# First plan unit by plain block products, six first tiles attended one at a time, later attention begun later

## The chip, the cores and the metric

One NeuronCore of a Trainium2 chip runs the whole program. The metric is the device time of one execution in microseconds (us). Engines have their own instruction queues, each in order: PE (TensorE), ACT (ScalarE), DVE (VectorE), POOL (GpSimd) and SP, which here only issues DMAs.

## What is computed

The reference, cut to what matters:

```python
# attention in chunks of 64 tokens: B=4, H=8, S=576, D=64
scores = scale * np.matmul(q_c, k_c.transpose(0, 1, 2, 4, 3))
scores = scores - np.max(scores, axis=-1, keepdims=True)
attn = np.exp(scores)
attn = attn / (np.sum(attn, axis=-1, keepdims=True) + 1e-09)
out = np.matmul(attn, v_c)
# x: 2304 x 512; four experts, 512 -> 1024 -> 512
for e in range(E):
    h = np.maximum(x @ w1[e], 0.0)
    out += p[:, e:e + 1] * (h @ w2[e])
# normalised by root mean square, then gated: 512 -> 1536 -> 512
g = xn @ w_gate
silu = g * (1.0 / (1.0 + np.exp(-g)))
return (silu * (xn @ w_val) @ w_out)
```

## The kernel before

The 2304 tokens are 18 tiles of 128, in three sets of six. A set is two token blocks of three tiles (384 columns, `NB`). For each set the expert layer runs eight **plan units** (`plan` in the main loop: four experts, two halves of the hidden features each), and after all sets the gated layer runs its units. Below, plan units are numbered through: 0 to 7 belong to set 0, 8 to 15 to set 1, 16 to 23 to set 2. A unit handles two feature pairs `fp`. Each is computed by `hidden` (L654), a Strassen-Winograd scheme over a two by two split of model halves and feature halves and of the two token blocks: seven products instead of eight, out of operands `x0` to `x9` and `w_0` to `w_6` that are sums of blocks. Every product is six matmuls, since each operand is kept as a high and a low part (float32r) and three of the four combinations are used (`PASSES`), for each of two halves of 128 rows. Then `outer` (L753) multiplies the hidden values by `w2`, 72 matmuls, and `flush` adds them up on DVE.

Operands of weights are made on the chip in set 0: `weights` (L301) takes raw w1 blocks, POOL forms sums (`tw`), ACT casts the high part, POOL subtracts to get the low part, and SP stores the result to DRAM for sets 1 and 2, which load it (`w1_load`). w2 is cast and subtracted in every set (`w2p`, four buffers). In sets 1 and 2, `decode` and `prepare` also turn the gated layer's float64 weights into such operands on DVE, POOL and ACT.

Attention handles two tiles at a time, a pair (`attention_unit`, L446): scores on PE into two PSUM banks, `mx` (maximum) and `e` (difference) on DVE, one exponential of 512 columns on ACT for each bank, `rs` (sum and reciprocal) on DVE, `at` (normalised) on POOL, transposition `trA` on PE, copy `aT` on ACT, value products `pv` on PE, copy to `xr`. `x_parts` then casts x operands.

The instructions stand in an order that the program itself works out while it is recorded. Work beside the products are generators ("chains") stepped by `Chains.tick` as the recorded PE time advances; `every` sets how often. Attention of set s+1 is such a chain, added at the start of set s; `norm` of set 0 is added at unit 10. Before unit 0 there is nothing to hide behind: `race` (L104) orders three attention pairs, the first x operands and the first weights by estimated costs in `yield {"ACT": 0.65}, 1` and the like, and fills expected PE idle time with transpositions of the identity into a spare bank (`idle`, dummies, 0.13 us each in its estimate). In it `begin` (L636) computes the two products of block 0 that need no sums; the rest of unit 0 follows when both blocks' operands exist.

## Time and profile before

| | us |
|---|---|
| median of 3 runs | 1272.42 (1272.21 to 1272.92) |
| profiled execution | 1270.46 |
| span in its profile, first to last instruction | 1268.7 |
| PE busy | 1230.4 |
| DVE, POOL, ACT busy | 809.8, 544.5, 413.0 |

The median is over executions without a profile being read; the profiled execution is one more. PE's busy time includes dummies, and matmuls overlap, so the start times in a timeline tell more than the durations.

### The profile page before, as it was taken

Reading aid. Unit: us, or ns where it says so; the run is one execution under the profiler, and the core shown is the slowest. Engines: PE = TensorE matmul, PEld = TensorE weight load, DVE = VectorE, ACT = ScalarE, POOL = GpSimd, SP = SyncE. Lnnn points to the kernel's source line nnn. Section 1 sums busy time; section 2 is a strip of 40 time slices with the busy share of each in tenths; the row PEclk is TensorE's granted clock in tenths of the full one; section 3 lists DMA queues with packets and bytes.
Section 4 is the critical chain, followed back from the end, with each engine's and each line's share of the span. In section 5 each row is a group of like instructions: output and inputs, shape, how many; then the busy total and the mean of one; then the engine's idle time right before and its main releaser. Section 6 shows DMA issues by size and latency. Waiting matters only on the chain. (4 is left out here: it accounts for less than half of the span.)

```text
span 1268.7 us, 20615 instructions
## 1 busy us (share of the span) xinstructions
PE 1230.4 (97%) x7323; PEld 1114.3 (88%) x7323; DVE 809.8 (64%) x1393; ACT 413.0 (33%) x924; POOL 544.5 (43%) x575
## 2 busy tenths in 40 slices
PE   8899999999997999999999999999999999999998
PEld 7788999989887888989998899898988989988997
DVE  6844344456676887767678666896658625763644
ACT  4434333334225232214242223143424232232211
POOL 5567666664345373527356255365204001131100
PEclk9999999999999999999999999999999999999999
DMA  8656555556577587655676766557856746765843
GB/s 285 223 169 218 188 191 181 201 167 205 202 268 239 163 292 261 207 191 213 234 254 204 279 228 229 192 171 303 271 171 239 258 132 224 244 204 200 284 139 125
DMA packets 139782, 274.30 MB, mean 216 GB/s; under 512 B 15648, under 2 KB 15648, under 8 KB 139680
## 3 DMA queue, kind: packets, MB, share of 16 engines
q1 hardware_dynamic: 139680, 272.99, 63.5%
q8 instruction: 58, 0.95, 0.3%
q14 instruction: 44, 0.36, 0.1%
HBM read 210.54 MB, written 62.39 MB: 215 GB/s over the span
## 5 line engine op out<-in xcount | busy, mean ns | idle before, releaser
L763 PE MATMUL o<-w,hh 128*128 128x512 f32 x1584 | 491.5, 391 | 4.0 <-ACT hh L703 2.2
L763 PEld LDWEIGHTS o<-w,hh 128*128 128x128 f32 x1584 | 295.1, 188 | 67.4 <-ACT hh L703 3.8
L763 PE MATMUL o<-w,hl 128*128 128x512 f32 x792 | 310.0, 391 | 1.5 <-DVE hl L200 0.3
L617 PE MATMUL d_ps<-x,w 128*128 128x384 f32 x1008 | 203.8, 338 | 9.8 <-DVE c_ps L201 9.8
L617 PE MATMUL a_ps<-x,w 128*128 128x384 f32 x1008 | 203.3, 337 | 7.3 <-ACT p L665 3.7
L200 POOL TENSOR_TENSOR w<-r,w 128x512 fp32r<-128x512 f32 (+1 forms) x144 | 162.6, 1139 | 103.0 <-ACT w L329 39.5
L617 PE MATMUL c_ps<-x,w 128*128 128x384 f32 x1008 | 203.1, 337 | 0.0
L617 PEld LDWEIGHTS d_ps<-x,w 128*128 128x128 f32 x1008 | 176.0, 188 | 12.9 <-DVE c_ps L201 11.3
L617 PEld LDWEIGHTS a_ps<-x,w 128*128 128x128 f32 x1008 | 176.8, 188 | 11.2 <-ACT p L665 4.3
L763 PEld LDWEIGHTS o<-w,hl 128*128 128x128 f32 x792 | 148.6, 188 | 37.7 <-DVE hl L200 5.3
L200 POOL TENSOR_TENSOR hl<-silu,hh 128x384 fp32r<-128x384 f32 x54 | 55.0, 1043 | 292.0 <-ACT hh L740 291.0
L617 PEld LDWEIGHTS c_ps<-x,w 128*128 128x128 f32 x1008 | 176.4, 188 | 0.2
L940 DVE SCALAR_TENSOR_TENSOR acc<-o,pr,acc 128x512 f32<-128x512 f32 x126 | 94.3, 749 | 126.9 <-PE o L763 126.8
L201 POOL TENSOR_TENSOR w<-w,sc 128x512 f32<-128x512 f32 x36 | 47.6, 1323 | 186.6 <-DVE sc L388 168.7
L200 POOL TENSOR_TENSOR w<-tw,w 128x256 fp32r<-128x256 f32 x112 | 90.8, 820 | 50.0 <-ACT w L233 50.0
L617 PE MATMUL b_ps<-x,w 128*128 128x384 f32 x504 | 101.9, 338 | 0.0
L703 ACT ACTIVATE hh<-c_ps 128x384 fp32r<-128x384 f32 x96 | 47.3, 493 | 158.4 <-DVE c_ps L201 158.3
L201 DVE TENSOR_TENSOR u<-b_ps,p 128x384 f32<-128x384 f32 x84 | 46.4, 553 | 81.9 <-PE b_ps L617 78.9
L201 DVE TENSOR_TENSOR u<-c_ps,u 128x384 f32<-128x384 f32 x84 | 46.7, 556 | 79.0 <-PE c_ps L617 78.5
L665 ACT COPY p<-a_ps 128x384 f32<-128x384 f32 x82 | 39.2, 478 | 165.1 <-PE a_ps L617 165.1
L233 ACT CAST w<-tw 128x256 fp32r<-128x256 f32 x112 | 42.4, 406 | 143.6 <-POOL tw L200 94.4
L617 PEld LDWEIGHTS b_ps<-x,w 128*128 128x128 f32 x504 | 88.9, 189 | 0.1
(98 smaller groups left out, 1349.6 us busy)
## 6 DMA issues: line engine op xcount, KB each, us to landing
w<-wgv SPq DMA_DIRECT2D x252, 256.0 KB, 3.9
w<-w1m SPq DMA_DIRECT2D x224, 256.0 KB, 5.2
r<-in_w SPq DMA_DIRECT2D x128, 256.0 KB, 4.8
w1m<-w SPq DMA_DIRECT2D x112, 256.0 KB, 2.2
wgv<-w SPq DMA_DIRECT2D x84, 256.0 KB, 4.8
raw<-in_wglu SPq DMA_DIRECT2D x36, 512.0 KB, 3.8
w<-wou SPq DMA_DIRECT2D x36, 512.0 KB, 7.3
wou<-q SPq DMA_DIRECT2D x24, 256.0 KB, 4.2
```

Source lines behind the costliest of these rows:

```text
L200: sub = lambda eng, o, a, b: eng.tensor_tensor(o, a, b, op=ALU.subtract)
L201: add = lambda eng, o, a, b: eng.tensor_tensor(o, a, b, op=ALU.add)
L233: nc.scalar.copy(halves(out[n])[:, 0], at[part_of[n]])
L617: nc.tensor.matmul(ps[:, :NB], wv[:, wi, k, :], xs[n][:, xi, k, :], start=(first and k == 0 and m == 0), stop=(last and k == KH - 1 and m ...
L665: nc.scalar.copy(p1, v(a))
L703: nc.scalar.activation(hi, src, AF.Relu)
L763: nc.tensor.matmul(ps, hs[fp, b, j][hx][:, r * P:(r + 1) * P], w2[2 * k + j][:, wi], start=((k, j, m) == (0, 0, 0)), stop=((k, j, m) == last),
L940: nc.vector.scalar_tensor_tensor(out=acc[i], in0=ps, scalar=pr[:, i, e:e + 1], in1=acc[i], op0=ALU.mult, op1=ALU.add,)
```

## The change

In set 0's first unit the eight plain block products replace the seven of the scheme (`plan` unit 0 only): `quarters` casts the four quarters of a raw w1 pair without any sum (POOL subtracts each low part), and `plain` multiplies them with x blocks 0, 1 (token block 0) and 9, 3 (token block 1). Block 0's products stand inside `race`, block 1's after it. `sums_of_first` makes and stores the four operands with sums (5, 4, 6, 3) of these two pairs later, as a chain. The x operands with sums are made by a chain too (`x_rest`), during unit 0's outer products.

The six first tiles are attended one at a time, and their loads are ordered by token block. `first_softmax` takes the maximum times minus the scale as the exponential's bias, straight from PSUM, in eight exponentials of 64 columns a tile, each with the sum over its columns written by ACT (`accum_out`). The value products' result is cast to the x operands' high part straight from PSUM by ACT, the low part is subtracted by DVE, and `xr` is copied behind that. `idle` counts 0.15 us a dummy.

The attention of set 1 begins at unit 1 instead of 0, that of set 2 at unit 12 instead of 8. The remaining hunks pass the pair's width through `attention_unit`, move the old softmax into a function, keep some buffers spare in `race` and let `x9` use `x2`'s buffer.

```diff
+    def quarters(fp, src):
+        last = None
+        for n, k, j in ((0, 0, 0), (1, 1, 0), (7, 0, 1), (2, 1, 1), (None,) * 3):
+            if last is not None:
+                yield {"POOL": 0.75}, 2
+                m, t, at = last
+                sub(nc.gpsimd, t[:, 1], at, t[:, 0].bitcast(F32))
+                parts["plain", fp, m] = t
+                users[id(t)] = 2
+                if m != 7:
+                    users[id(t)] += 1
+                    work.add(store(t, w1m[0][fp][:, m], (0, fp, m)))
+            if n is not None:
+                yield {"ACT": 0.4}, 2
+                t, at = w1p.get(f"w1_{n}"), src[j][:, k * 2 * P:(k + 1) * 2 * P]
+                nc.scalar.copy(t[:, 0], at)
+                last = n, t, at
+    def sums_of_first():
+        for fp in list(kept):
+            def stored(n, t, fp=fp):
+                work.add(store_q(t, halves(t), w1m[0][fp][:, n], (0, fp, n)))
+            yield from operands(kept[fp], tp, stored, (5, 4, 6, 3))
+            tp.put(*kept.pop(fp))
     def weights():
         for s in range(NSET):
-                    for order in () if s > 0 else (ORDER,) if (e, u) != (0, 0) else ((0, 1), (5, 4, 6, 3, 2)):
-                        for fp in own:
-                            key, where = ("moe", s, e, fp), w1m[e][fp]
-                            if order[0] == 0:
-                                kept[fp] = yield from fetched()
-                            def stored(n, t, key=key, where=where):
-                                users[id(t)] = 2
-                                parts[(*key, n)] = t
-                                work.add(store(t, where[:, n], (*key[2:], n)))
-                            yield from operands(kept[fp], w1p, stored, order)
-                            if order[-1] == ORDER[-1]:
-                                tp.put(*kept.pop(fp))
+                    for fp in own if s == 0 else ():
+                        ts = yield from fetched()
+                        if (e, u) == (0, 0):
+                            kept[fp] = ts
+                            yield from quarters(fp, ts)
+                            continue
+                        key, where = ("moe", s, e, fp), w1m[e][fp]
+                        def stored(n, t, key=key, where=where):
+                            users[id(t)] = 2
+                            parts[(*key, n)] = t
+                            work.add(store(t, where[:, n], (*key[2:], n)))
+                        yield from operands(ts, w1p, stored)
+                        tp.put(*ts)
                     for f in range(2 * UF * u, 2 * UF * (u + 1)):
                         raw, = yield from fetched()
                         while not w2p.free():
                             yield
                         t = w2p.get("w2")
+                        yield {"ACT": 0.6}, 1
                         nc.scalar.copy(t[:, 0], raw)
-                        yield
+                        yield {"POOL": 1.3}, 1
                         sub(nc.gpsimd, t[:, 1], raw, t[:, 0].bitcast(F32))
                         tp.put(raw)
 ...
-    def attention_unit(u, loaded=None):
+    def attention_unit(u, loaded=None, done=None):
 ...
+        if done:
+            yield from first_softmax(sc, ex, att[0])
+        else:
+            yield from softmax(sc, ex, att, mx, G, rows, d)
 ...
+        if done:
+            b, t = divmod(u[0] % TPS, TPB)
+            pieces = []
+            for n in range(2):
+                for k in range(2):
+                    x, o = xs[((0, 1), (9, 3))[b][k]], t * P + n * CH
+                    src = ps[n][:, k * KH * CH:(k + 1) * KH * CH].rearrange("p (k n) -> p k n", k=KH)
+                    pieces.append([src, *(x[:, m, :, o:o + CH] for m in range(2))])
+            for n, (src, hi, _) in enumerate(pieces):
+                yield {"ACT": 0.22}, 1 + n
+                nc.scalar.copy(hi, src)
+            for src, hi, lo in pieces:
+                yield {"DVE": 0.22}, len(pieces)
+                sub(nc.vector, lo, src, hi.bitcast(F32))
+            done()
 ...
+    def first_softmax(sc, ex, att):
+        mx, nb, rs = (sm.tile([P, 2, HP], F32, tag=f"f{n}", name=n) for n in ("mx", "nb", "rs"))
+        for h2 in range(2):
+            nc.vector.tensor_reduce(
+                mx[:, h2, :].unsqueeze(2), sc[h2][:, :HP * CH].rearrange("p (g n) -> p g n", n=CH), axis=AX.X, op=ALU.max
+            )
+            yield {"DVE": 0.45 if h2 == 0 else 0.2}, 1
+        nc.vector.tensor_scalar(nb, mx, -SCALE, None, op0=ALU.mult)
+        for h2 in range(2):
+            yield {"ACT": 0.9}, 1
+            for g in range(HP):
+                cols = slice(g * CH, (g + 1) * CH)
+                nc.scalar.activation(
+                    ex[h2][:, cols], sc[h2][:, cols], AF.Exp, scale=SCALE, bias=nb[:, h2, g:g + 1],
+                    accum_out=rs[:, h2, g:g + 1],
+                )
+            banks.put(sc[h2])
+        yield {"DVE": 0.5}, 1
+        nc.vector.tensor_scalar_add(rs, rs, 1e-9)
+        nc.vector.reciprocal(rs, rs)
+        for h2, e in enumerate(ex):
+            yield {"POOL": 0.65}, 1
+            nc.gpsimd.tensor_tensor(
+                att.rearrange("p (hp r n) -> p hp r n", hp=HP, r=2)[:, :, h2, :],
+                e[:, :HP * CH].rearrange("p (g n) -> p g n", n=CH),
+                rs[:, h2, :].unsqueeze(2).to_broadcast([P, HP, CH]),
+                op=ALU.mult,
+            )
+            tp.put(e)
 ...
+    first_w, made_plain = {}, []
+    def plain(fp, b, use, last):
+        for j in range(2):
+            names = ((0, 7), (1, 2))
+            while not banks.free() or any((fp, names[k][j]) not in first_w for k in range(2)):
+                for k in range(2):
+                    key = ("plain", fp, names[k][j])
+                    if key in parts:
+                        first_w[key[1:]] = parts.pop(key)
+                yield {}, 1
+            ps = bank("c_ps")
+            for k in range(2):
+                yield {"PE": 1.1}, 1
+                product(ps, first_w[fp, names[k][j]], ((0, 1), (9, 3))[b][k], k == 0, k == 1)
+            catch_up()
+            if len(made_plain) > 1:
+                yield {"ACT": 0.5}, 2
+                made_plain.pop(0)()
+            made_plain.append(lambda j=j, ps=ps: use(b, j, ps))
+        while last and made_plain:
+            yield {"ACT": 0.5}, 1
+            made_plain.pop(0)()
+            catch_up()
 ...
-        tiles = [attention_tiles(u) for u in own(0)]
-        for u, ts in zip(own(0), tiles):
-            attention_dma(u, ts, (0, 1))
-        for u, ts in zip(own(0), tiles):
-            attention_dma(u, ts, (2,))
+        lead = [[i] for i in range(TPS)]
+        tiles = [attention_tiles(u) for u in lead]
+        for group in (range(TPB), range(TPB, len(lead))):
+            for k in group:
+                attention_dma(lead[k], tiles[k], (0, 1))
             work.step(fetching)
-        first = [attention_unit(u, ts) for u, ts in zip(own(0), tiles)]
+            for k in group:
+                attention_dma(lead[k], tiles[k], (2,))
         nc.sync.dma_start(out=pr, in_=probs)
         nc.sync.dma_start(out=gb, in_=gvec.partition_broadcast(P))
 ...
+        def unit(k):
+            yield from attention_unit(lead[k], tiles[k], lambda: ended.add(k))
+        def block(b):
+            mine = range(TPB) if b == 0 else range(TPB, len(lead))
+            while not all(k in ended for k in mine):
                 yield {}, 1
-            yield from x_sum(n)
-            yield from x_parts(n, eng, True)
-        def two_blocks(t):
-            engines = {5: nc.vector, 4: nc.vector, 6: nc.vector, 3: nc.gpsimd, 2: nc.vector}
-            return [(operand(n, eng), t + 0.8 * m, None) for m, (n, eng) in enumerate(engines.items())]
+            for fp in range(UF) if b == 0 else ():
+                yield from plain(fp, 0, moe_use(fp), fp == UF - 1)
         scratch = banks.get("scratch")
-        waited = []
         def idle(us):
-            for _ in range(int(us / 0.13)):
+            for _ in range(int(us / 0.15)):
                 nc.tensor.transpose(scratch[:, :P], ident, ident)
-        def until():
-            if 5 in xs and all(key in begun for key in early) and not waited:
-                waited.append(True)
-                return True
+        arrive = [3.5, 5.7, 7.6, 14.5, 16.0, 17.5]
+        spared[0] = 5
         gen = work.race(
-            [
-                (first[0], 4.4, None),
-                (first[1], 8.6, lambda t: [(one_block(), t, None)]),
-                (first[2], 12.0, two_blocks),
-            ],
-            (weights(), 15.0, None),
+            [(unit(k), arrive[k], None) for k in range(len(lead))]
+            + [(block(0), 10.0, None), (block(1), 20.0, None)],
+            (weights(), 9.0, None, 0.2),
             idle,
-            until,
         )
+        spared[0] = 0
         banks.put(scratch)
-        x_done()
         feeding = work.add(gen, 0.5)
+        def x_rest():
+            for n in (5, 4, 6):
+                yield from x_sum(n)
+                yield from x_parts(n, nc.vector, True)
+            yield from x_sum(2)
+            while not plain_done:
+                yield
+            yield from x_parts(2, nc.vector, True)
+            x_done()
+        for o in (4, 5, 6, 2):
+            tmp[o] = [tp.get(f"s{o}_{k}") for k in range(KH)]
+        for i in range(TPS):
+            acc[i] = tp.get(f"acc_{i}")
+        plain_done = []
+        resting = work.add(x_rest(), 0.9)
+        work.add(sums_of_first(), 1.6)
 ...
-            if moe and s + 1 < NSET:
-                ahead = work.add(attention(own(s + 1)), first=True)
             for k, (e, fps) in enumerate(plan):
                 end = k == len(plan) - 1
+                if moe and (s, k) == (0, 1) and resting in work.chains:
+                    work.force(resting, lambda: resting not in work.chains)
                 room[0] = 6 if k == 0 else 8 if k >= len(plan) - 2 else 0
+                if moe and (s, k) in ((0, 1), (1, 4)):
+                    ahead = work.add(attention(own(s + 1)), first=True)
 ...
-                    if moe:
+                    if moe and (s, k) == (0, 0):
+                        for _ in plain(fp, 1, moe_use(fp), fp == fps[-1]):
+                            pass
+                        if fp == fps[-1]:
+                            plain_done.append(True)
+                    elif moe:
```

PE from the first products of unit 0; `c_ps`, `a_ps`, `b_ps` are their PSUM banks, `w_n` operand n, `scratch` the dummies. Before:

```order
L617 MATMUL a_ps<-x_534,w_0_361 128x384 x6
L868 MATMUL scratch<-ident 128x128 x5
L617 MATMUL a_ps<-x_601,w_1_410 128x384 x6
L868 MATMUL scratch<-ident 128x128 x13
L617 MATMUL a_ps<-x_534,w_0_464 128x384 x6
L868 MATMUL scratch<-ident 128x128 x5
L617 MATMUL a_ps<-x_601,w_1_523 128x384 x6
L868 MATMUL scratch<-ident 128x128 x13
L617 MATMUL b_ps<-x_689,w_5_592 128x384 x6
```

Now, from the last tile's value products on:

```order
L706 MATMUL c_ps<-x_187,w_0_438 128x384 x6
L706 MATMUL c_ps<-x_188,w_1_634 128x384 x6
L956 MATMUL scratch<-ident 128x128
L706 MATMUL c_ps<-x_187,w_7_711 128x384 x6
L706 MATMUL c_ps<-x_188,w_2_714 128x384 x6
L706 MATMUL c_ps<-x_189,w_0_357 128x384 x6
L706 MATMUL c_ps<-x_190,w_1_403 128x384 x6
L706 MATMUL c_ps<-x_189,w_7_424 128x384 x6
L706 MATMUL c_ps<-x_190,w_2_434 128x384 x6
L706 MATMUL c_ps<-x_189,w_0_438 128x384 x6
L706 MATMUL c_ps<-x_190,w_1_634 128x384 x6
L706 MATMUL c_ps<-x_189,w_7_711 128x384 x6
```

Block 0's four products of the second pair and the eight of block 1 now follow one another with one dummy between them; those of the first pair stand earlier, between the last tiles' transpositions and value products.

ACT from the second weight cast on (`w_0_438` is the first quarter of the second pair, read from `r_0_178`):

```order
L315 CAST w_1_403<-r_0_165 128x256
L315 CAST w_7_424<-r_1_166 128x256
L315 CAST w_2_434<-r_1_166 128x256
L315 CAST w_0_438<-r_0_178 128x256
L560 CAST x_187<-pv_406 128x2x64
L560 CAST x_188<-pv_406 128x2x64
L560 CAST x_187<-pv_407 128x2x64
L560 CAST x_188<-pv_407 128x2x64
L526 COPY aT_445<-trA_440 128x512
L571 COPY xr<-pv_406 128x4x64
L625 ACTIVATE e_426,rs<-sc_383,nb 128x64 x4
L560 CAST x_187<-pv_459 128x2x64
```

and SP's queue around that raw block:

```order
L471 DMA qk_a_156<-in_qkv 128x512
L471 DMA qk_b_157<-in_qkv 128x512
L253 DMA r_0_178<-in_w 128x512
L253 DMA r_1_179<-in_w 128x512
L471 DMA v_152<-in_qkv 128x512
```

The cast of `w_0_438` stands ahead of the second tile's x operands, and its load behind those of the last qk tile.

POOL from unit 0's w2 operands (`w` of 128x512) to unit 1. Before:

```order
L200 TENSOR_TENSOR w_3_876<-tw_629,w_3_876 128x256
L200 TENSOR_TENSOR w_2_925<-r_1_180,w_2_925 128x256
L200 TENSOR_TENSOR w_929<-r_185,w_929 128x512
L200 TENSOR_TENSOR w_952<-r_796,w_952 128x512
L200 TENSOR_TENSOR w_972<-r_798,w_972 128x512
L200 TENSOR_TENSOR w_990<-r_809,w_990 128x512
L509 TENSOR_TENSOR at_921<-e_919,rs_986 128x4x64
L509 TENSOR_TENSOR at_922<-e_919,rs_986 128x4x64
```

Now:

```order
L197 TENSOR_TENSOR w_719<-r_717,w_719 128x512
L197 TENSOR_TENSOR w_772<-r_770,w_772 128x512
L197 TENSOR_TENSOR tw_809<-r_1_166,r_0_165 128x256
L197 TENSOR_TENSOR tw_809<-r_1_166,tw_809 128x256
L197 TENSOR_TENSOR tw_810<-r_1_166 128x256
L197 TENSOR_TENSOR w_901<-r_802,w_901 128x512
L197 TENSOR_TENSOR w_905<-r_804,w_905 128x512
L197 TENSOR_TENSOR tw_925<-r_1_818,r_0_817 128x256
L197 TENSOR_TENSOR tw_925<-r_1_818,tw_925 128x256
L197 TENSOR_TENSOR tw_926<-r_1_818 128x256
```

The last two w2 operands of unit 0 now stand behind two sums of the first pair and right ahead of the first operands of unit 1.

## Rows read from the trace of the kernel before

**Rows 1.** Windows, plan units 0-3, 8-10, 12: length, busy PE, PEld, DVE, ACT, POOL; clock; DMA.

```profile
31.28:80.72 49.44, 43.25 (x331) 37.00 (x330) 31.09 (x53) 18.97 (x46) 30.92 (x37) 0.97 0.53 185
80.72:118.28 37.56, 36.85 (x357) 32.61 (x356) 19.85 (x37) 15.13 (x37) 25.96 (x35) 1.00 0.70 237
118.28:152.40 34.12, 34.12 (x229) 30.72 (x228) 16.63 (x32) 14.02 (x34) 23.42 (x31) 1.00 0.58 195
152.40:183.30 30.90, 30.90 (x158) 28.07 (x157) 13.83 (x24) 11.19 (x28) 20.62 (x26) 1.00 0.47 157
307.81:345.24 37.43, 35.96 (x294) 31.47 (x293) 24.49 (x46) 10.25 (x21) 11.44 (x12) 1.00 0.64 223
345.24:384.55 39.31, 36.85 (x358) 32.65 (x356) 29.43 (x52) 12.88 (x29) 21.46 (x25) 1.00 0.69 238
384.55:428.98 44.43, 36.62 (x229) 32.23 (x228) 32.60 (x60) 17.13 (x40) 18.70 (x20) 0.96 0.62 199
459.88:491.71 31.83, 31.59 (x158) 27.87 (x156) 23.84 (x37) 9.90 (x23) 20.02 (x20) 1.00 0.79 273
```

**Rows 2.** Timeline of PE: start and length in us; in brackets idle time and releaser.

```profile
3.52 0.71 PE L468 MATMUL sc<-qk_a 64*64 64x64 f32 x16 [3.52 <-DMA qk_a<-in_qkv]
...
17.54 2.95 PE L868 MATMUL scratch<-ident 128*128 128x128 f32 x25
...
28.47 3.06 PE L868 MATMUL scratch<-ident 128*128 128x128 f32 x26
...
41.04 1.31 PE L617 MATMUL a_ps<-x,w 128*128 128x384 f32 x6 [3.57 <-ACT p L645]
...
54.21 0.46 PE L468 MATMUL sc<-qk_a 64*64 64x64 f32 x16
...
55.30 1.32 PE L617 MATMUL c_ps<-x,w 128*128 128x384 f32 x6
```

**Rows 3.** Waits of PE between 300 and 430 us: total, times, longest.

```profile
PE a_ps L617 <- ACT p L665: 3.3, 1, 3.3
PE trA L525 <- POOL at L509: 2.5, 1, 2.5
```

**Rows 4.** A window of 3.4 us in unit 0 (columns as in rows 1).

```profile
42.30:45.70 3.40, 3.40 (x17) 3.40 (x16) 3.06 (x7) 1.40 (x3) 0.97 (x1) 0.50 0.86 265
```

**Rows 5.** SP's timeline and DMA view (us to landing) at 10.9 us: the 18th load.

```profile
10.93 0.33 SPq L444 DMA_DIRECT2D v<-in_qkv  x1
...
v<-in_qkv SPq DMA_DIRECT2D x1, 256.0 KB, 6.5
```

**Rows 6.** Timeline of ACT at 399 us: an activation that sums.

```profile
398.95 0.64 ACT L791 ACTIVATE sq<-acc 128x512 f32<-128x512 f32 x1
399.48 0.20 ACT L791 ACTIVATION_READ_ACCUMULATOR sq<-acc 128x1 f32 x1
399.57 0.49 ACT L703 ACTIVATE hh<-a_ps 128x384 fp32r<-128x384 f32 x1
```

**Rows 7.** Timeline of ACT at 15 us.

```profile
15.39 0.40 ACT L233 CAST w<-r 128x256 fp32r<-128x256 f32 x1
15.70 0.63 ACT L500 ACTIVATE e<-e 128x512 f32<-128x512 f32 x1
```

**Rows 8.** Timeline of DVE, first attention.

```profile
7.68 0.69 DVE L482 TENSOR_REDUCE mx<-sc 128x8 f32<-128x512 f32 x1 [7.68 <-PE sc L468]
...
11.04 0.17 DVE L505 TENSOR_SCALAR rs<-rs 128x8 f32<-128x8 f32 x1
```

**Rows 9.** Groups of POOL by form (busy, mean ns); the last for 24 to 43 us.

```profile
L200 POOL TENSOR_TENSOR w<-r,w 128x512 fp32r<-128x512 f32 x96 | 126.6, 1331 | 83.3 <-ACT w L329 39.5 <-PE b_ps L617 38.2 <-DMA r<-in_w 2.5
L200 POOL TENSOR_TENSOR w<-tw,w 128x256 fp32r<-128x256 f32 x112 | 90.8, 820 | 50.0 <-ACT w L233 50.0
...
L509 POOL TENSOR_TENSOR at<-e,rs 128x256 f32<-128x256 f32 x36 | 21.9, 634 | 34.7 <-DVE rs L506 30.6 <-issue 3.7 <-PE pv L546 0.4
...
L200 POOL TENSOR_TENSOR w<-tw,w 128x256 fp32r<-128x256 f32 x7 | 6.8, 1003 | 0.0
```

More of the change, by code (lines that the diff above doesn't have):

```diff
@@ L574, in x_part, with x_tile_of @@
         return xr[:, b, kd + k, :]
+    def x_tile_of(n):
+        xs[n] = xsp.tile([P, 2, KH, NB], F32R, tag=f"x{2 if n == 9 else n}", name=f"x{n}")
+        return xs[n]
     def x_sum(n):
         for o, *_ in x_made.get(n, ()):
[L579 removed]
+            if o not in tmp:
+                tmp[o] = [tp.get(f"s{o}_{k}") for k in range(KH)]
         for k in range(KH):
```

176 lines of the change are left out of this document (78 added, 98 removed).

## The prediction, made before the changed kernel ran

> **What bounds the kernel now.** The page's totals come first (the table): PE is busy 1230.4 of 1268.7 us, so a gain can only come from stretches in which PE waits, or fills time with dummies. The windows by plan unit show where these lie [rows 1]. A plan unit with nothing beside it takes 30.90 us; that is PE's own pace: 84 x 384 columns of products and 72 x 512 of outer products, 0.447 ns a column, so 1.03 us a product of six matmuls and 0.229 an outer matmul. Unit 0 takes 49.44 us and begins only at 31.28. Units 8, 9 and 10, which carry the attention of set 2, take 37.43, 39.31 and 44.43 us. The timeline of PE [rows 2] shows what fills the first 31 us: 2.95 us of dummies (x25) between two tiles' work, 3.06 us more before the first product, then a wait of 3.57 us on a ScalarE copy. The first product of unit 1 starts at 80.72, the end of unit 0's window.
>
> What an attention pair costs PE itself: its scores stand from 54.21 to 55.30, 1.1 us [rows 2]; transpositions and value products alone make unit 2 longer than unit 3, by 34.12 - 30.90 = 3.2 [rows 1]. Together 4.3 us. Unit 0 has one such pair of set 1 in it.
>
> In units 8 to 10 the work beyond three plain units is 121.17 - 92.70 = 28.5 us; three pairs are 12.9, so 15.6 us are lost. The waits there [rows 3] name a copy on ScalarE and GpSimd's `at`, both on in-order engines that also carry the weight preparation. Unit 10 alone loses 10.3 (44.43 - 30.90 - 3.2), partly at a lower clock, 0.96 in the mean.
>
> **The start, walked through.** The new order is followed with durations of the rows. Loads keep their pace in SP's queue: the 18th, now the first half of the second raw weight pair, stands where a v stood, and lands at 10.9 + 6.5 = 17.4 [rows 5].
>
> ScalarE becomes the busiest engine of the start. Its new cost is 48 exponentials of 64 columns, each with a sum to read out. No row shows this form. Lower end: start to start, 512 columns take 0.53 and the read-out 0.09 [rows 6], 256 columns 0.31 [rows 7]; the line through these gives 0.145 for 64, with the read-out 0.23 a group. Upper end: nothing overlaps, 0.41 for 256 less 192 columns at 0.86 ns, plus 0.20: 0.45. The rows hold neither a bias from memory nor so short an exponential, so I take the middle, **0.34 a group, 2.7 us a tile**. The Trainium skill, "ScalarE: Activation LUTs", section "What ACT_TABLE_LOAD costs", says that a bias read through a pointer adds about 93 ns to an ACTIVATE, and it speaks against cutting one long instruction into eight; by its figures a group is (estimate) 0.24 + 0.10 = 0.34, and the sum would be 2.3 us worse than by the rows' lower end. No run here shows it yet.
>
> Other prices: maximum of 256 columns 0.43 on DVE, 0.69 for 512 less 256 columns at 1 ns, and 0.17 to 0.2 for a small instruction [rows 8]; GpSimd's normalisation 0.6 a half [rows 9]; aT copy 0.5; a 128-column cast 0.2 and a 256-column copy 0.3, start to start, on the line above.
>
> - Tile 0: scores from 3.5 to 5.0 (a group of qk_a took 0.71 there, 0.46 at 54 us [rows 2]); maximum and bias to 6.1; exponentials to 8.9; sums' reciprocal 9.4; GpSimd 10.6; PE's dummies end 11.8; transposition 12.3; aT waits for half of tile 2's exponentials, 13.5; values 14.6.
> - Tiles 1 and 2 end their value products at 17.5 and 20.3. Their casts share ScalarE with the first weights.
> - Tile 3's exponentials end at 23.0, tiles 4 and 5 at 26.0 and 28.8. Block 0's first products run from 22.6 and fill PE between transpositions.
> - Value products of tiles 3, 4, 5 end at 30.4, 31.5 and 34.3, held by aT copies at 29.3 and 32.9.
> - Then four products of block 0 are left, to 38.5, and block 1's eight, to 46.8.
> - The outer products need the third and fourth w2 operand, which ScalarE casts only after the last relu (its queue holds them there). Cast from 47.7, GpSimd 1.3 each: ready at 49.6 and 50.9. Six matmuls in, at 48.2, PE waits 1.4, three later 0.6: 2.0 in all. The 72 outer matmuls take 16.5.
>
> Unit 0 so ends at 46.8 + 2.0 + 16.5 = 65.3. Before it was 80.72 with a pair of 4.3 in it, so the start gains 80.72 - 4.3 - 65.3 = **11.1 us**, the two extra products (2.1 us: 16 instead of 14) being inside.
>
> The sum takes back some. The walk counts no hand-off between engines; no row isolates one, and I allow 0.05 for each of some 25 links of its last chain: 1.3 us. After unit 0, GpSimd has 38 instructions to the last w2 operand of unit 1, 34 of 0.82 and 4 of 1.33 [rows 9], 33.2 us: from 50.9 to 84.1. PE wants that operand at 65.3 + 14.5 products + 1.1 scores + 2.1 = 83.0. So 1.1 us are lost there; set 1's attention, now spread over units 1 to 3, loses what it lost in units 1 and 2 (71.68 - 61.80 - 8.6 = 1.3). SP's stores of three plain operands per pair and of four late sums stand behind loads needed long after; I cost them at nothing, the cover being PE's 30 us per unit; without it a late load would hold a cast and with it ScalarE's whole queue. The buffers kept spare and x9's place in x2's buffer cost nothing either: x2 is made during unit 0's outer products and wanted 6 us after them. **Start: 11.1 - 1.3 - 1.1 = 8.7 us.**
>
> **Set 2's attention, begun in unit 12 instead of 8.** The same 15.6 us are in question. Unit 8, where one pair meets decoding alone, loses 37.43 - 30.90 - 4.3 = 2.2; unit 9 loses 3.0 with the scores of two pairs; unit 10, where the norm of set 0 joins them, loses 10.3. Unit 12 has DVE busy 23.84 us without attention [rows 1]; a pair adds some 4.8 (six instructions over 512 columns of 0.69, four small ones [rows 8]) and 4.3 to the unit's length. That makes 0.79 to 0.81 of its time, against 0.65, 0.75 and 0.73 in units 8 to 10. No norm stands there. I take 2.6 a unit, the mean of units 8 and 9, and 1 us for the norm left alone: 15.6 - 8.8 = **6.8 us** gained. Ends: 13.6 if pairs lose as little as in units 1 and 2 (0.65 each), and -15.3 if each costs unit 10's 10.3.
>
> **Sum.** 8.7 + 6.8 = 15.5 us. The profiled execution took 1270.46 (span 1268.7 and 1.8 around it), so 1255.0; the median of the runs stands 1.96 above that execution, so **1256.9**.
>
> **Rivals.**
> - *Set 2's attention stays as dear.* For it: DVE at 0.8 in unit 12, above what it had in units 8 to 10. Against: no norm. Then 8.7 alone: 1263.7.
> - *GpSimd starves units 1 and 2.* Its subtractions took 1.0 where DVE worked beside it [rows 9], against 0.82. 34 x 0.2 = 6.8 us later, and nothing hides it: 1263.7.
> - *Short exponentials cost like long ones.* 0.64 + 0.20 = 0.84 a group [rows 6]. The walk moves 2.3 us per 0.11, so 10.4 us: 1267.3. Overlap in the same rows speaks against it.
> - *PE's clock falls in the start.* Dummies, counted in the order, drop from 123 to 41, and the walk leaves PE waiting 1 to 1.5 us at a time between 17 and 34 us. Before, a wait of 3.57 us was followed by 3.40 us at granted 0.50 [rows 2, 4]. Each such stretch costs up to 1.7 us of products; three of them give 1262.0. The Trainium skill, "TensorE: Matmul & The Clock Gate", section "What's actually happening", has idleness bring the clock to its lower level; by that rule the trace agrees, at 0.50 after the wait.
> - *Slower:* each of the three moved pairs costs what unit 10 cost. GpSimd's normalisation then stands in its queue behind a late DVE sum, the weight casts stand behind GpSimd, and the copy of a_ps stands behind the casts on ScalarE; PE waits for it. 3 x 10.3 = 30.9, against 15.6: 15.3 worse, less 8.7: 1279.0. It decides from 8.1 us a unit (24.3 in all).
> - *The change does not shorten the start,* because the loads bound it: the last v stands four places behind the load that lands at 17.4, and PE has 12.9 us of attention and 16.5 of products to do. Then only set 2 gains, 1265.6. The walk's path lies on ScalarE after 20, not on loads, so this gets little.
>
> **How the numbers follow.** Forecast 0.52; set 2 as dear 0.14; GpSimd 0.10; clock 0.12; long exponentials 0.05; no shorter start 0.02; slower 0.05. A measurement of this kernel tells some 0.2%, 2.5 us, from no change. All but the slower case are faster by more; where two of the dear ones meet (set 2 as dear with long exponentials: 1274.1) the time is the same as before, and I take 0.03 of their 0.43 for it. Faster 0.92, same 0.03, slower 0.05. The range: upwards it takes in all rivals but the slower one, to 1267. Downwards, with 0.23 a group (2.3 us) and 4 of the 6.8 us more that set 2 may give: 1250.
>
> **What would show it.** Right: the first outer product near 47 us and unit 1's first product near 65 to 67; exponential plus read-out 0.25 to 0.4 us start to start; PE waiting on a POOL w operand at the first outer products; units 8 to 11 near 31 us but for some norm, 12 to 14 near 38. Wrong: unit 1 beginning after 72; a granted clock of 0.50 before 40 us; waits over 8 us in one of units 12 to 14; long idle times of ScalarE in the start, which would say that something else led.

## The result, and the profile after

| | before | after |
|---|---|---|
| median of 4 runs | 1272.67 us (1272.21 to 1274.28) | 1250.20 us (1249.67 to 1250.31) |
| profiled execution, span | 1270.46, 1268.7 us | 1250.31, 1248.5 us |
| ratio, 95% interval | | 0.9825 [0.9809, 0.9840] |

Faster by 22.5 us where 15.5 were forecast; the time lies 0.2 us inside the lower end of the range, 1250 to 1267. On another chip later the changed kernel took 1251.13, ratio 0.9847 [0.9832, 0.9863].

Windows of the changed kernel by plan unit, first product to first product: units 0, 1, 10, 12, 13, 14, 19 and 23 (columns as in [rows 1]).

```profile
22.39:64.09 41.70, 39.45 (x279) 34.59 (x280) 27.89 (x58) 24.42 (x89) 27.68 (x33) 1.00 0.46 159
64.09:102.48 38.39, 36.34 (x294) 31.68 (x292) 18.71 (x35) 16.06 (x39) 34.55 (x47) 1.00 0.77 264
360.78:396.36 35.58, 31.94 (x158) 27.90 (x156) 32.12 (x53) 14.48 (x36) 18.63 (x18) 1.00 0.71 244
427.30:462.92 35.62, 35.62 (x293) 31.58 (x292) 30.84 (x50) 14.15 (x29) 23.13 (x25) 1.00 0.92 330
462.92:501.40 38.48, 36.46 (x293) 31.53 (x292) 28.16 (x50) 12.06 (x25) 16.55 (x17) 1.00 0.72 250
501.40:537.28 35.88, 35.74 (x294) 31.72 (x292) 21.77 (x39) 10.84 (x23) 13.83 (x16) 1.00 0.57 199
663.63:694.71 31.08, 31.08 (x157) 27.99 (x156) 23.78 (x42) 8.87 (x19) 13.61 (x13) 1.00 0.77 279
790.34:821.46 31.12, 31.12 (x157) 28.06 (x156) 26.72 (x43) 12.13 (x25) 13.34 (x10) 1.00 0.45 136
```

Unit 1 begins at 64.09 instead of 80.72 [rows 1], and unit 4, with set 1's attention done in both kernels, at 173.95 instead of 183.30: **the start and set 1 gave 9.35 us.** Units 8 to 14 took 238.5 us instead of 245.7: **7.2 us**, set 2's attention now in 12 to 14. Units 15 to 23 took 284.2 instead of 288.5: **4.3 us** that no step foresaw (unit 19: 34.45 before; unit 23: 33.15; unit 15 grew from 32.88 to 33.51). The rest is 0.6 us longer; a unit with nothing beside it takes 30.95 us instead of 30.89, and no run shows why.

ScalarE's timeline at the first exponentials of the changed kernel:

```profile
5.90 1.28 ACT L625 ACT_TABLE_LOAD   x1 [5.90 <-DVE nb L620]
7.19 0.32 ACT L625 ACTIVATE e<-sc,nb 128x64 f32<-128x64 f32 x1
7.40 0.19 ACT L625 ACTIVATION_READ_ACCUMULATOR e<-sc,nb 128x1 f32 x1
7.50 0.31 ACT L625 ACTIVATE e<-sc,nb 128x64 f32<-128x64 f32 x1
```

From one exponential to the next, its read-out between them, it is 0.31 us here and 0.29 in the mean (the ninth starts at 9.52). But the table load, done at 0.73 us in the kernel before, stands behind the wait for the first bias, on the path.

TensorE's timeline, first product and first stalls at the outer products:

```profile
22.39 2.36 PE L706 MATMUL c_ps<-x,w 128*128 128x384 f32 x12 [0.25 <-ACT e L625]
...
45.58 0.63 PE L856 MATMUL o<-w,hh 128*128 128x512 f32 x2
...
48.65 0.50 PE L856 MATMUL o<-w,hh 128*128 128x512 f32 x1 [0.91 <-POOL w L197]
...
49.89 0.50 PE L856 MATMUL o<-w,hh 128*128 128x512 f32 x1 [0.26 <-POOL w L197]
```

The outer products begin at 45.58 (near 47 forecast) and wait for GpSimd's `w`, the w2 operand, as the prediction had it.

### The profile page after: what moved, and what is told of

It reads as the page before. It is cut to its first block, busy times and chain, and to the rows that moved or that the text cites. A ratio compares the mean times of both kernels' runs of the same rounds, so it can differ in the third digit from the quotient of the medians.

```text
span 1248.5 us, 20621 instructions
## 1 busy us (share of the span) xinstructions
PE 1222.0 (98%) x7253; PEld 1105.6 (89%) x7253; DVE 798.6 (64%) x1406; ACT 428.2 (34%) x1037; POOL 538.5 (43%) x575
## 4 chain that ended last, share of the span: by engine, by line
PE 81%; DVE 9%; DMA 3%; ACT 2%; issue 2%; POOL 1%; SPq 0%; DVEq 0%; POOLq 0%; ACTq 0%
PE o L856 40%; PE d_ps L706 11%; PE a_ps L706 11%; PE c_ps L706 11%; PE b_ps L706 6%; DVE silu L830 2%; DVE c_ps L198 1%; DVE u L198 1%; PE pv L544 1%; DMA qk_b<-in_qkv 1%; DMA w1m<-w 1%; POOL w L197 1%; DMA w<-wgv 1%; PE xT L910 1%; DVE d_ps L198 1%
## 5 line engine op out<-in xcount | busy, mean ns | idle before, releaser
L706 PE MATMUL c_ps<-x,w 128*128 128x384 f32 x1080 | 216.1, 336 | 0.2 <-ACT e L625 0.2
L706 PE MATMUL d_ps<-x,w 128*128 128x384 f32 x984 | 198.8, 336 | 6.8 <-DVE c_ps L198 6.8
L706 PE MATMUL a_ps<-x,w 128*128 128x384 f32 x984 | 198.7, 336 | 1.3 <-ACT p L759 1.3
L706 PEld LDWEIGHTS c_ps<-x,w 128*128 128x128 f32 x1080 | 188.8, 188 | 0.8 <-ACT e L625 0.5
L856 PEld LDWEIGHTS o<-w,hl 128*128 128x128 f32 x792 | 148.6, 188 | 38.5 <-DVE hl L197 4.7
L706 PEld LDWEIGHTS d_ps<-x,w 128*128 128x128 f32 x984 | 172.1, 188 | 9.2 <-DVE c_ps L198 9.1
L706 PEld LDWEIGHTS a_ps<-x,w 128*128 128x128 f32 x984 | 173.4, 188 | 4.6 <-ACT p L759 1.9
L197 POOL TENSOR_TENSOR w<-tw,w 128x256 fp32r<-128x256 f32 x112 | 87.5, 790 | 39.4 <-ACT w L231 39.4
L706 PE MATMUL b_ps<-x,w 128*128 128x384 f32 x492 | 99.0, 335 | 0.0
L706 PEld LDWEIGHTS b_ps<-x,w 128*128 128x128 f32 x492 | 86.4, 188 | 0.1
```

What stands on the lines that cost most here:

```text
L197: sub = lambda eng, o, a, b: eng.tensor_tensor(o, a, b, op=ALU.subtract)
L706: nc.tensor.matmul(ps[:, :NB], wv[:, wi, k, :], xs[n][:, xi, k, :], start=(first and k == 0 and m == 0), stop=(last and k == KH - 1 and m ...
L856: nc.tensor.matmul(ps, hs[fp, b, j][hx][:, r * P:(r + 1) * P], w2[2 * k + j][:, wi], start=((k, j, m) == (0, 0, 0)), stop=((k, j, m) == last),
```

## The experiments

Unit lengths below are from the profiles' PE timelines, as above. Where a span moves further than the edited stretch, the units that moved are named.

### Where set 2's attention stands, with the new start and with the old

`set2_back`, an edit of the changed kernel, and `only_set2`, of the kernel before:

```diff
# set2_back
-                if moe and (s, k) in ((0, 1), (1, 4)):
+                if moe and (s, k) in ((0, 1), (1, 0)):
# only_set2
-            if moe and s + 1 < NSET:
+            if moe and s == 0:
                 ahead = work.add(attention(own(s + 1)), first=True)
...
+                if moe and (s, k) == (1, 4):
+                    ahead = work.add(attention(own(s + 1)), first=True)
```

> The changed kernel with set 2's attention begun in unit 8 again, as before the change; all else is kept. Theory: the later place is worth what units 8 to 14 gained from before to after, 7.2 us (245.7 us then, 238.5 now), so 1250.2 + 7.2 = 1257.4; if the waits of 2.8 and 1.6 us that units 19 and 23 lost with the change also hang on it, up to 4.3 us more, 1261.7. Rival: the place is worth nothing, and these units gained because something else of the change took work off their engines; then the time stays within 2.5 us of 1250.2 and units 8 to 10 stay below 35 us.

> The kernel before with one edit: set 2's attention begins in unit 12 instead of unit 8. Theory: 1272.5 less 7.2 = 1265.3, and 1261.0 if the waits in units 19 and 23 go with it; unit 1's first product stays at 80.7 us, as nothing of the start is touched. Rival: the later place pays only beside the new start; the time stays within 2.5 us of 1272.5. Third: set 2's attention costs the same anywhere, units 12 to 14 then lose 15.6 us as units 8 to 10 did, and the time is again that of before.

Measured: set2_back 1253.12 us, ratio 0.9863 [0.9848, 0.9878]; only_set2 1264.46, ratio 0.9951 [0.9936, 0.9966], unit 1 from 80.77. With the two kernels they make a square (us, spans of the profiles):

| | units 8 to 14 | units 15 to 23 |
|---|---|---|
| old start, set 2 from unit 8 (before) | 245.7 | 288.5 |
| old start, set 2 from unit 12 (only_set2) | 240.0 | 287.6 |
| new start, set 2 from unit 8 (set2_back) | 241.5 | 284.5 |
| new start, set 2 from unit 12 (after) | 238.5 | 284.2 |

Windows of set2_back, units 8 to 10:

```profile
299.87:337.33 37.46, 36.00 (x293) 31.50 (x292) 24.82 (x46) 10.35 (x21) 11.60 (x12) 1.00 0.64 223
337.33:375.52 38.19, 36.92 (x357) 32.69 (x356) 28.56 (x52) 12.78 (x29) 21.79 (x25) 1.00 0.74 244
375.52:417.38 41.86, 37.07 (x229) 32.33 (x228) 33.05 (x60) 17.23 (x40) 19.01 (x20) 0.96 0.64 212
```

All rivals fall: the later place pays by itself, in units 8 to 14 5.7 us with the old start and 3.0 with the new (in only_set2 unit 7 took 1.1 us more, 32.97). But my 7.2 was too much: at the old place units 9 and 10 are 1.1 and 2.6 us shorter than in [rows 1] with nothing changed there but the start. By their sums the 4.3 us of units 15 to 23 hang on the new start (4.0 and 3.4), not on set 2 (0.9 and 0.3), but the sums hide what the units did:

| | unit 15 | unit 19 | unit 23 |
|---|---|---|---|
| before | 32.88 | 34.45 | 33.15 |
| only_set2 | 34.83 | 31.63 | 33.08 |
| set2_back | 32.73 | 31.59 | 31.43 |
| after | 33.51 | 31.08 | 31.12 |

Unit 23 goes with the start. Unit 19 does not: the later place of set 2 with the old start, and the new start with the old place, each shorten it by 2.8 us or more, and only_set2 lost most of that again in unit 15, where a stretch at granted clock 0.50 lies from 557.4 us. (Set2_back's start also had a stretch at granted clock 0.50, unit 1 at 65.58, which is not its edit's doing.)

What those 4.3 us are, unit 19 first: SP's and VectorE's timelines of the kernel before, then of the changed kernel,

```profile
670.32 12.23 SPq L356 DMA_DIRECT2D raw<-in_wglu  x2
682.64 0.86 SPq L426 DMA_DIRECT2D wgv<-w  x2
...
685.02 1.01 SPq L426 DMA_DIRECT2D wgv<-w  x2
```

```profile
691.51 1.40 DVE L374 TENSOR_SCALAR w<-raw 128x512 uint32<-128x512 uint32 x1 [3.16 <-DMA wgv<-w]
```

```profile
654.70 12.23 SPq L383 DMA_DIRECT2D raw<-in_wglu  x2
667.02 1.40 SPq L453 DMA_DIRECT2D wgv<-w  x3
...
670.43 0.42 SPq L453 DMA_DIRECT2D wgv<-w  x1
```

```profile
674.73 0.61 DVE L401 TENSOR_SCALAR w<-raw 128x512 uint32<-128x512 uint32 x1
```

The row x2 on SP spans two issues; the second stood until one of the decoder's two raw buffers came free, and the stores `wgv<-w` behind it in SP's queue left only then. VectorE's next decode step writes into a buffer that such a store still reads. In the kernel before that is the fourth store: issued at 685.58 us, it landed at 691.43, and VectorE waited 3.16 us, with TensorE's sums queued behind it. After the change SP stands just as long (12.23 us in both), and the stores leave as late in the unit. What differs is that the step now stands two instructions later in VectorE's order (so in all other profiles, only_set2's too), and that the fourth store landed 4.2 us after its issue instead of 5.9, at 674.65: the step begins 0.08 us after it. That was luck in part. In the eleven profiles with the new start and set 2 in units 12 to 14 the order is the same, the step waited between 0 and 1.9 us, and unit 19 took from 31.06 to 33.53 us.

In unit 23 the kernel before has three decode steps among the sums that make the next x (at 809.69, 810.14 and 814.36 us) and TensorE waits 1.60 us; in the changed kernel none stands there.

### The start: the softmax's form, and the dummies

```diff
# old_softmax
-            yield from first_softmax(sc, ex, att[0])
+            yield from softmax(sc, ex, att, mx, G, rows, d)
# no_dummies, in idle(us)
-            for _ in range(int(us / 0.15)):
-                nc.tensor.transpose(scratch[:, :P], ident, ident)
+            return
```

> The changed kernel with its six first tiles' softmax in the old form: maximum taken off by VectorE, two exponentials of 256 columns without bias, sums by VectorE; tiles still singly and unit 0 still in plain products. Theory: the bias form moves some 10 us of work from VectorE to ScalarE (48 groups of 0.29 us on ScalarE against 12 exponentials of 0.31; on VectorE a shift and a sum of 0.38 us a half and two small instructions more a tile), and ScalarE was the busier engine of the start, so that the old form costs little: VectorE's 26 us are done by 33 us if nothing holds them, and the time is 1250 to 1254. Rival: the bias form is the core of the gain, because VectorE's chain of shift and sum lies on each tile's path; then unit 1 begins 5 us or more after 64.1, and the time is 1255 or more.

> The changed kernel without the 41 dummy transpositions that fill TensorE's waits in the start. Theory: none of the waits they fill is as long as the 3.57 us after which the granted clock fell to 0.50 in the kernel before (the longest is 1.9 us), so the clock stays at 1.0, unit 1 begins at 64.1 and the time is 1250.2 within 2.5 us. Rival: without them the granted clock falls to 0.50 in the first 40 us; each product of 1.03 us that runs there takes twice that, and with a stretch of 3.4 us, as in the kernel before, unit 1 begins 1.7 us later, with two such stretches 3.4: 1251.9 to 1253.6.

Measured: old_softmax 1254.09, ratio 0.9868 [0.9853, 0.9882]; unit 1 begins at 67.94, 3.9 us later, and the span is 4.2 longer. That is the upper end of my theory, short of the rival; in its start the granted clock stood at 0.50 from 19.5 to 22.9 us, so part of the 3.9 may be the clock's. The order of the whole start is worked out anew with other costs, so the 3.9 are not the exponentials' alone.

no_dummies: 1254.85, ratio 0.9872 [0.9855, 0.9888]. Unit 1 begins 1.0 us later, at 65.06. TensorE's timeline without dummies, then with them:

```profile
11.50 1.12 PE L521 MATMUL trA<-ident,at 128*128 128x128 f32 x4 [2.49 <-POOL at L635]
13.74 1.97 PE L544 MATMUL pv<-aT,v 64*64 64x64 f32 x32 [1.13 <-ACT aT L526]
```

```profile
11.50 0.66 PE L521 MATMUL trA<-ident,at 128*128 128x128 f32 x4
11.99 0.93 PE L956 MATMUL scratch<-ident 128*128 128x128 f32 x7
13.74 1.15 PE L544 MATMUL pv<-aT,v 64*64 64x64 f32 x32 [0.82 <-ACT aT L526]
```

Without dummies the first tile's matmuls take nearly twice as long (1.97 against 1.15), up to 17.6 us. The clock's records, at 1.00, begin at 18.1 us here and at 10.7 in the changed kernel, so none covers these rows, but the durations speak for the lower level of the clock, 1.2 GHz. The rival was right in kind, 1.0 us in size. The other 4 us came elsewhere, in units with the same order of work: 1.5 in unit 13, with a stretch at 0.50 that the changed kernel did not have, and 2.4 in unit 19, where the fourth store landed late.

### How far the changed kernel repeats itself, and three repairs

```diff
# table_early
         make_identity(nc, ident)
+        warm = sm.tile([P, 1], F32, tag="warm", name="warm")
+        nc.scalar.activation(warm, ident[:, :1], AF.Exp)
# w2_early
         feeding = work.add(gen, 0.5)
+        work.force(feeding, lambda: ("w2", "moe", 0, 0, 3) in parts)
# norm_late (the norm of set 0; that of set 1 keeps its place)
-                if k == 2 and (s == 0) != moe:
-                    work.add(norm(s - 1 if moe else NSET - 1), 1.5)
+                if (kind, s, k) in (("moe", 2, 2), ("moe", 2, 4), ("glu", 0, 2)):
+                    work.add(norm({2: 1, 4: 0}[k] if moe else NSET - 1), 1.5)
```

> The changed kernel as it is, once more, on the chip of the three edits beside it. Theory: part of its gain hangs on how work happens to meet. Units 15 to 23 gained 4.3 us that no step foresaw (units 19 and 23 lost their waits of 2.8 and 1.6), and the four kernels run so far lose between 0.1 and 2.5 us in unit 19 with one order of VectorE's work there; so its execution here differs from 1250.2 by 1 to 3 us, and units 10, 13 or 19 by as much, while unit 1 begins at 64.1 again. Rival: nothing of it is chance; every unit is within 0.3 us of the first profile and the time within 1 us of 1250.2.

> The changed kernel with one more exponential, of one column, ahead of everything on ScalarE, so that the table load of 1.28 us runs while the first loads are under way and not at 5.90, behind the wait for the first bias. Theory: that load is on the path of the start, since ScalarE is then busy with hardly a gap to 28 us; the first exponential begins at 5.9 instead of 7.2, unit 1 at 62.8 to 63.2 instead of 64.1, and the time is 1 us less than that of the changed kernel beside it. Rival: the raw weights and the loads of tiles 3 to 5 set the pace after the second tile; unit 1 begins at 64.1 still.

> The changed kernel with the casts of the third and fourth w2 operand of unit 0 put behind the second one on ScalarE, where it was idle from 38.4 to 42.1 us, and GpSimd's two subtractions with them. Theory: the waits of 0.91 and 0.26 us at the first outer products go, as the prediction had it that these operands come late because ScalarE casts them behind the last relu; unit 1 begins at 62.9 and the time is 1.2 us less. Rival: the two subtractions of 1.28 us only push back the sums for unit 1's weights on GpSimd, and what unit 0 gains is lost at the end of unit 1: its wait of 1.46 us at 83.7 grows to over 2.5 and the time is the same.

> The changed kernel with the normalisation of set 0 in unit 20 instead of unit 10; that of set 1 stays in unit 18, where unit 18 took 30.95 us, as a unit with nothing beside it does. Theory: in unit 10 the norm, which the prediction priced at 1 us, cost 4.6 (35.58 less 30.95), as VectorE's short instructions on 6 columns stood at 1.2 us instead of 0.17 while GpSimd ran, and a table load of 1.28 us stood between them; where this meets nothing it costs nothing. Unit 10 then takes 31 us, unit 20 31 to 32, and the time is 3.6 to 4.6 less than that of the changed kernel beside it. Rival: the norm costs about 4 us wherever VectorE also decodes, and unit 18 was the lucky one; unit 20 takes 35 us and the time is the same.

| run | median us | ratio, interval | unit 1 | span |
|---|---|---|---|---|
| after_again | 1251.13 | 0.9847 [0.9832, 0.9863] | 63.96 | 1247.6 |
| table_early | 1249.79 | 0.9838 [0.9823, 0.9853] | 63.77 | 1251.9 |
| w2_early | 1249.98 | 0.9844 [0.9826, 0.9862] | 61.88 | 1247.6 |
| norm_late | 1249.72 | 0.9837 [0.9822, 0.9852] | 63.99 | 1248.3 |

**after_again** speaks for the rival: units 10, 13 and 19 came within 0.1 us of the first profile, and only unit 1 differed by more than 0.3 (37.76 against 38.39). So the lucky places came out alike in two executions. Whether they always do is not shown: its four runs range from 1249.71, the profiled one, to 1251.94.

**table_early**: the first exponential moved to 5.99, as meant, and the start gained 0.2 to 0.3 only. (Its profiled execution is the slowest of its five: units 10, 13 and 19 took 36.83, 40.07 and 33.53, hence the long span.) Its ScalarE timeline:

```profile
17.19 0.40 ACT L315 CAST w<-r 128x256 fp32r<-128x256 f32 x1 [0.84 <-DMA r<-in_w]
17.50 0.76 ACT L560 CAST x<-pv 128x128 fp32r<-128x128 f32 x4
18.14 0.62 ACT L526 COPY aT<-trA 128x512 f32<-128x512 f32 x1
```

The rival held: a weight cast waits for the load that I had put at 17.4 [rows 5], and tile 2's copy stands behind it, at 18.14 (18.41 in the changed kernel).

**w2_early**: the waits at the outer products are gone, 72 of them take 16.4 us instead of 18.5, and unit 1 begins 2.1 earlier. Yet the span is that of after_again. The window of its unit 13, at a mean granted clock of 0.96, shows where 1.5 of it went (0.4 more went in unit 1):

```profile
460.54:500.57 40.03, 38.00 (x294) 32.76 (x292) 28.14 (x50) 12.07 (x25) 16.54 (x17) 0.96 0.69 241
```

**norm_late**: unit 10 fell from 35.58 to 32.18, but unit 20 rose to 33.09 and unit 19 to 32.29: by the profiles nothing is left. Unit 19's part is not the norm's: there the decode step waited 1.36 us once more, as the fourth store landed 12.3 us into the unit instead of 11.0. Why unit 10 pays is seen in the changed kernel, VectorE, GpSimd and TensorE at the same time:

```profile
373.31 0.17 DVE L891 TENSOR_TENSOR z<-y 128x6 f32<-128x6 f32 x1
373.51 0.17 DVE L892 TENSOR_TENSOR z<-z,ms 128x6 f32<-128x6 f32 x1
373.71 1.24 DVE L893 TENSOR_SCALAR z<-z 128x6 f32<-128x6 f32 x1
374.98 1.18 DVE L894 TENSOR_TENSOR y<-y,z 128x6 f32<-128x6 f32 x1
376.08 0.55 DVE L198 TENSOR_TENSOR u<-c_ps,u 128x384 f32<-128x384 f32 x1
```

```profile
373.64 1.28 POOL L197 TENSOR_TENSOR w<-r,w 128x512 fp32r<-128x512 f32 x1 [1.33 <-ACT w L356]
374.88 1.26 POOL L198 TENSOR_TENSOR w<-w,sc 128x512 f32<-128x512 f32 x1
```

```profile
377.29 1.31 PE L706 MATMUL d_ps<-x,w 128*128 128x384 f32 x6 [2.80 <-DVE c_ps L198]
```

The norm's short steps, and a table load of 1.28 us on ScalarE between them, stand ahead of the sum that frees TensorE. Two steps on six columns each last as long as the GpSimd instruction beside them.

### What table_early and norm_late left open, set 1's place, and all together

```diff
# cast_later: table_early, and in quarters(fp, src)
+            if (fp, n) == (1, 0):
+                yield {"LOAD": 2.0}, 1
             if n is not None:
# norm_16, in place of the same two lines as norm_late
+                if (kind, s, k) in (("moe", 2, 0), ("moe", 2, 2), ("glu", 0, 2)):
+                    work.add(norm((0 if k == 0 else 1) if moe else NSET - 1), 1.5)
# set1_back
-                if moe and (s, k) in ((0, 1), (1, 4)):
+                if moe and (s, k) in ((0, 0), (1, 4)):
# all_four: cast_later, w2_early and norm_16
```

> The changed kernel with the early exponential of the run table_early and the casts of the second weight pair behind tile 5's exponentials instead of ahead of tile 2's copy of aT. Theory: of the 1.2 us that the early table load gave the first exponentials, 1.0 was lost in that cast, which waited 0.84 us for its load until 17.19 us with tile 2's copy behind it on ScalarE. With the cast moved the copy stands at 16.9, and unit 1 begins at 62.7 to 63.0 (63.77 in table_early, 64.0 in the two profiles of the changed kernel). Rival: the last of these casts comes at 33.4 now, and its product waits for it and for GpSimd's subtraction behind it; unit 1 begins at 63.7 or later.

> The changed kernel with the normalisation of set 0 in unit 16 instead of unit 10. Theory: what the norm costs hangs on how full VectorE is in its unit. It cost 4.6 us in unit 10 (VectorE busy 0.98 of it), 2.1 in unit 20 (0.95 of it with the norm, 0.79 without), nothing in unit 18 (0.87 with it). Unit 16 has VectorE at 0.62 and takes the norm for 0 to 0.5; unit 10 takes 32.2, as in norm_late; the time is 3 us less than the 1250.2 to 1251.1 of the changed kernel. Rival: the time is the same within 1.5 us, since what unit 10 gives brings decoding's work forward, and a load of the decoder that arrives late costs it again in unit 19 (32.3 in norm_late, 31.1 in the two profiles of the changed kernel).

> The changed kernel with set 1's attention begun in unit 0, as before the change. The prediction priced this part of the change at nothing: set 1 was to lose 1.3 us beyond its products wherever it stands. Theory: its first pair now meets the end of the start, where ScalarE is busy for 0.85 of unit 0 and GpSimd for two thirds; the pair's casts and its normalisation hold up the w2 operands and the weights of unit 1, and units 0 to 3 together take 2 to 5 us more; 1252 to 1256. Rival: the later place costs, not gains, since in units 1 to 3 GpSimd is busy for 34.5 of 38.4 us and they lose 4.1 us beyond their three pairs; with it in unit 0 units 0 to 3 are 1 to 2 us shorter.

> The changed kernel with four edits together: the early exponential, the casts of the second weight pair later, the third and fourth w2 operand earlier, and the normalisation of set 0 in unit 16. Theory: they lie on different stretches and add up: 1.1 us of the start, 2.1 of unit 0 (as w2_early's profile shows), 3.4 of unit 10, 6.6 in all: 1244 to 1245. Rival: the later units fill in, as they did in w2_early and norm_late, where 2.1 and 3.4 us gained in a unit were worth 0 in the span: unit 13 with a stretch at granted clock 0.50 (1.5 us) and unit 19 with the late load (up to 2.5); then 1247 to 1250.

| run | median us | ratio, interval | unit 1 | span |
|---|---|---|---|---|
| cast_later | 1247.74 | 0.9822 [0.9804, 0.9840] | 62.98 | 1246.4 |
| norm_16 | 1249.83 | 0.9837 [0.9820, 0.9854] | 63.97 | 1247.8 |
| set1_back | 1253.91 | 0.9871 [0.9851, 0.9890] | 72.19 | 1250.5 |
| all_four | 1245.21 | 0.9804 [0.9787, 0.9821] | 61.16 | 1243.2 |

**cast_later**: tile 2's copy stands at 17.08, unit 1 at 62.98: the queue behind the waiting cast had held it, as expected.

**norm_16**: unit 10 gives 3.4 us again, and unit 16, where VectorE had the most room, takes 3.0 back. My theory that VectorE's fullness sets the price falls. Its VectorE timeline in unit 16, and TensorE's:

```profile
578.04 0.54 DVE L198 TENSOR_TENSOR u<-b_ps,p 128x384 f32<-128x384 f32 x1
...
579.90 1.24 DVE L893 TENSOR_SCALAR z<-z 128x6 f32<-128x6 f32 x1
...
581.74 0.54 DVE L198 TENSOR_TENSOR u<-c_ps,u 128x384 f32<-128x384 f32 x1
```

```profile
582.93 1.31 PE L706 MATMUL d_ps<-x,w 128*128 128x384 f32 x6 [1.95 <-DVE c_ps L198]
```

As in unit 10 the short steps fall between two sums of the last product group. In unit 18, which pays nothing, they come after its last sum, from 651.23 us, while TensorE does outer products; but GpSimd is idle there too, until 654.75, and no step is stretched. So the place within the unit, or GpSimd beside it, decides; which of the two is not shown, as a norm held back to that place was not tried.

**set1_back**: units 0 to 3 together take 153.8 us (after 151.6, after_again 150.9). By these profiles the later place is worth 2.2 to 2.9 us, so pricing it at nothing was wrong. The longest new wait, in unit 0, is TensorE's own for the pair's normalisation on GpSimd, 3.2 us, with a stretch at 0.50 behind it; it is not one for weights or w2 operands, as I had it.

**all_four** is faster than both kernels: unit 4 begins at 170.72, 2.5 to 3.2 earlier. Its five runs, 1244.84 to 1246.62, lie below all eight of the changed kernel. The theory comes nearer, though the norm's part came to 0.4 instead of 3.4; unit 13 was spared the lower clock (38.46). That its time was met is in part luck: the edited stretches gave 2.9 to 3.7 us of the 6.6, and 1.5 to 1.6 of the 4.5 to 5.3 us in the span lie in no edited stretch. Units with nothing beside them took 30.89 us, as in the kernel before, table_early and cast_later, and not 30.95; the cause is open.

## Why the prediction came out as it did

Direction, order of the parts and signs held; the 6.7 us between 1256.9 and 1250.2 are, by the profiles, 0.65 in the start, 0.4 in units 8 to 14, 4.3 in units 15 to 23 and 2.1 between profile and median, less 0.6 elsewhere. The range allowed downwards for shorter exponentials and for more from set 2; most of the 6.7 came from neither, so it is luck that the time still fell inside, by 0.2 us.

- **The walk of the start: right in mechanism, some 2.5 us too slow.** Tiles 0 to 2 ended their value products at 14.9, 17.7 and 20.2 (14.6, 17.5, 20.3 forecast), block 0 began at 22.39 (22.6), the outer products at 45.58 (46.8, with 1.3 for hand-offs 48.1). Two terms are mis-sized. The exponential group took 0.29, not 0.34: 2.4 us less on ScalarE over 48 groups, which moves the walk's end by 1.0, at its own 2.3 us per 0.11. And the 1.3 allowed for hand-offs do not show. Against them the walk left out the table load, 1.28, which cost the start 0.2 to 0.3 by table_early and 1.0 to 1.1 with the casts that cast_later moves; what is then left of the 2.5 is open. Tile 5's value products ended at 32.90 (34.3), and from there twelve products followed almost without a wait. ScalarE was the busiest engine as said: it was busy from 7.2 to 28.6 us without a gap of note. The trace gives neither the rows' 0.23 nor the 0.34 estimated from the Trainium skill, "ScalarE: Activation LUTs", section "What ACT_TABLE_LOAD costs": it is 0.195 from an exponential to its read-out and 0.095 on.
- **The w2 operands: right.** 2.0 us forecast, 18.5 - 16.4 = 2.1 measured; w2_early removed them.
- **After unit 0: too cheap.** Units 1 to 3 lost 109.9 - 92.9 - 12.9 = 4.1 us, where 1.1 + 1.3 were allowed, even at the later place of set 1, which was priced at nothing and gave 2.2 to 2.9. The wait at unit 1's outer products (1.46) was for a relu on ScalarE, not for a w2 operand. Together with the walk: 9.35 against 8.7.
- **Set 2: the sum right, its parts not.** Units 12 to 14 lost 110.0 - 92.9 - 12.9 = 4.2 us (1.4 a unit, 2.6 taken), and unit 10 lost 4.6 where 1 was taken for the norm: 8.8 in both sums, by luck. Of the 4.6 the norm itself is 3.4 (norm_late); the other 1.2 had no term. And only 3.0 to 5.7 of the 7.2 us come from the place; the step failed that put all of the 15.6 us down to what stands in units 8 to 10.
- **Units 15 to 23: no step.** 4.3 us: 3.4 in unit 19, which hang on the place of one decode step and on when one store lands, and 2.0 in unit 23, which go with the new start, less 0.6 in unit 15 and 0.5 elsewhere.
- **From the profiled execution to the median.** 1.96 us were added because before's median stood that far above its profiled execution; after's stands 0.1 below.

Of the rivals: set 2 stayed dear is out (units 12 to 14 at 35.6 to 38.5); long exponentials are out (0.29); GpSimd was busy for 34.55 of unit 1's 38.39 us but TensorE waited for it only once in units 1 to 3, for 0.5 us; loads did not bound the start, though table_early ran into one at once. In the changed kernel's profile no stretch at 0.50 is recorded in the start, so the clock rival failed; no_dummies shows that 41 dummies still did their work. Not tested: which part of the start's gain comes from the plain products, which from the single tiles and which from the order of the loads, since no run takes one of these back alone.

## What to carry to other kernels

On an in-order queue look not only for what is slow but for what waits: a cast for its load, a table load behind a wait for data, short dependent steps ahead of the sum that frees another engine. A term measured in one stretch is partly the phase in which the work meets there, so test a moved part with the rest old and with the rest new, and compare stretches, not only times: two sums of stretches can agree, or a square come out clean, while the units inside them moved in opposite ways.

## What the runs showed of the hardware

- The table load, 1.28 us, stood behind the first exponential's wait; one exponential on a constant tile brought it from 5.90 back to 0.73 us.
- A six-column VectorE instruction took 1.24 us instead of 0.17 while GpSimd ran one of 1.28. The Trainium skill, "SBUF — State Buffer", section "SBUF: two separate sides", says of a VectorE instruction in a two-port mode or with two inputs in SBUF that the port pair it shares with GpSimd is held for a whole instruction and blocks the other fully; the trace agrees, 0.17 becoming 1.24, and each of the two stretched steps ended within 0.03 us of the GpSimd instruction beside it.
- The lower clock after a wait is not a fixed price. Unit 10 took 35.58 us in one execution of the changed kernel without a stretch at 0.50 and 35.57 in another with one, from 376.8 us: the 0.5 and 0.4 us that TensorE waited at the outer products in the first are gone in the other. In unit 13, after waits of 2.0 us in all, it came in four of the eleven profiles with the new start and set 2's attention there, and cost 1.5 us (40.0 to 40.1 instead of 38.5).
